# A new written-out order for an attention and gated-MLP kernel on one core, with its last half tile stored from ScalarE's queue

## The chip, the cores and the metric

The kernel runs on one core of a Trainium2 chip. The metric is the device time of one execution in microseconds, smaller is better. Before the change, three runs gave 280.32, 282.18 and 282.18, median 282.18.

## What is computed

Eight batches of twelve-head attention (448 positions, 64 per head) with RMS-normalised q and k, followed by a gated MLP over the 768 joined channels. Cut to what matters:

```python
q_n, k_n = rmsnorm(q, g_q), rmsnorm(k, g_k)
attn = softmax(q_n @ k_n.T / 8)          # per batch and head, 448 x 448
x = (attn @ v) laid out as [8, 448, 768]
h = np.maximum(x @ w_in, 0.0)            # 768 -> 1024
u, v = h[..., :512], h[..., 512:]
v_n = (v - mean(v)) / sqrt(var(v) + 1e-6)
v_s = w_spatial @ v_n + b_spatial[:, None]   # mixes the 448 positions
out = (u * v_s) @ w_out                  # 512 -> 768, float32
```

## The kernel before

A group is four heads of one batch, so there are 24 groups (0 to 23) of three per batch. A group's scores are worked out in seven units, each followed by one exponential over 128x896 numbers. Every engine does part of each group:

- SyncE's queue (SP) loads q, k and v of a group (words `l`, `L`, 224 KB or 448 KB each, into ten `raw` buffers), issues the transposing DMAs (`T`) and the stores (`t`).
- ScalarE (ACT), VectorE (DVE) and GpSimd (POOL) share squares (`q`, `Q`), normalising (`n`, `N`) and casting v (`F`); DVE sums the squares (`r`, `R`), ACT makes the reciprocal root of them with a Ln and an Exp (`i`, `j`, `I`, `J`).
- TensorE (PE) transposes the first groups (`p`, `P`), whose results an engine copies out of PSUM (`k`, `K`); later groups go through `T`, and their k through a scaling (`Z`).
- PE makes scores (`S.group.unit`, eight small matmuls that run side by side), ACT exponentiates them (`E`), and PE sums them in passes: `s` for the sums of the softmax, `a` and `b` for the two halves of attention times v. A pass serves two groups with eight small matmuls when its last number is 1, one group with four when it is 0. `D`, `d` and `X` divide.
- The MLP of a batch: `V`, `W` and `U` (times w_in), `c`, `B`, `M`, `m`, `A` (normalising), `u`, `H` and `G` (mixing and gating), `O`, `W` (times w_out), `o` (copy out of PSUM), `t` (store).
- GpSimd's queue loads the weights: `ws` the 448x448 mixing matrix, which PE transposes in four steps (`Y`), `wi` w_in in eight parts, `wo` w_out. `wb` and `wx` bring the bias. `z.n` is n matmuls without use, which only keep PE working.

No loop and no planner runs in the kernel: the string `PLAN` lists some 1640 words, and one pass over it records each word's instructions. An engine works through its own words in that order and never overtakes, and a DMA is issued when its engine's queue comes to it. A word reads `name.args/slots/engine`: `S.9.0/45` puts unit 0 of group 9 into PSUM banks 4 and 5, `E.9.0/8/a` exponentiates it on ACT into buffer 8, `Q.2.1/0/g` squares k (index 1; q is 0) of group 2 on POOL (`a` ACT, `v` DVE). Groups 0 and 1 have passes of their own, the others are summed in pairs. Three lines of the order, around groups 8 to 10:

```python
H.1.1/2 I.13//a L.15.1/1 F.8//g J.13//a E.8.4/e/a X.6.1 L.17.0/9 S.9.0/45 G.1.1 S.9.3/67 N.11.0/3/g L.10.2/2 H.1.3/3
E.9.3/2/a H.1.2/0 E.9.0/8/a G.1.3 N.13.1/0/g S.9.2/12 L.17.1/7 G.1.2 S.10.3/67 s.8.3.1/34 E.9.2/7/a T.11.0/3 s.8.0.1
R.12.1 s.8.4.1 b.8.1.1/05 s.8.1.1 E.10.3/3/a b.8.3.1 S.10.4/12 N.13.0/2/g R.14.1 b.8.5.1 s.8.5.1 E.10.4/i/a s.8.2.1
```

Of the kernel before, what the change touches and what calls it, by code (L numbers as in the profile page):

```python
# [22 lines left out]
l.0.1/0 setup l.1.1/1 l.1.0 z.32/0 gl.1//a l.0.0 gl.0//a L.1.1/2 L.1.0/3 L.3.1/4 q.0.1/0/g L.2.1/5 L.2.0/6 ws  # L23
q.1.1/1/a L.3.0/7 L.4.1/8 r.1.1 L.0.2/9 r.0.1 q.1.0//v i.1//a j.1//a n.0.1//v q.0.0//a r.1.0 p.0.1/0 gA n.1.1//v gB/1
r.0.0 p.1.1/2 gC k.0.1/0/v i.0//a z.4/3 j.0//a k.1.1/0/v n.0.0//g Q.1.0/2/a S.0.3/01 wi.1.2 L.5.0/0 p.0.0/2 Q.1.1/1/a
n.1.0//g R.1.0 z.2/3 E.0.3/0/a L.4.0/1 p.1.0/3 R.1.1 Q.3.1/0/a z.7/4 Q.2.1/2/g k.0.0//v I.1//a k.1.0//v Q.2.0/1/a
S.0.1/01 S.0.4/23 S.0.5/45 J.1//a S.0.0/67 E.0.4/1/a R.2.0 N.1.0/0/g E.0.0/2/a S.0.2/23 R.2.1 E.0.5/3/a L.6.1/3
P.1.0/6 N.1.1/1/v I.2//a E.0.2/4/a S.0.6/45 K.1.0/1/v L.1.2/2 P.1.1/7 Q.3.0/1/g E.0.6/5/a Y.3/6 K.1.1/1/v J.2//a
E.0.1/6/a R.3.1 S.1.0/23 N.2.1/2/g S.1.2/45 E.1.0/7/a Y.1/7 R.3.0 E.1.2/8/a S.1.3/01 N.2.0/3/v L.7.1/5 S.1.6/23 I.3//a
P.2.1/4 E.1.3/9/a F.0//v L.6.0/6 P.2.0/5 J.3//a Q.4.1/2/a y.1//v N.3.0/0/g K.2.1/2/v S.1.4/01 E.1.6/a/a Y.2/7 y.3//v  # L30
K.2.0/2/v E.1.4/b/a Q.4.0/0/g S.2.3/23 T.3.0/3 y.2//v b.0.3.0/4 S.1.5/56 R.4.1 E.2.3/c/a s.0.2.0/7 a.0.5.0/0 a.0.3.0
s.1.6.0/1 E.1.5/d/a s.0.1.0 L.7.0/9 S.2.1/23 Q.6.1/1/g R.4.0 s.1.2.0 s.0.0.0 L.5.1/7 E.2.1/e/a S.1.1/56 s.1.3.0
a.0.1.0 s.1.4.0 E.1.1/f/a s.1.0.0 S.2.6/23 wi.1.1 N.3.1/1/v s.0.4.0 s.0.6.0 I.4//a b.0.1.0 E.2.6/g/a S.2.4/56 a.0.4.0
s.0.3.0 F.1//v L.2.2/4 b.0.2.0 E.2.4/h/a s.1.5.0 Q.5.0/2/v s.0.5.0 L.8.0/2 a.0.0.0 b.0.4.0 S.2.0/23 J.4//a D.0/0/a
s.1.1.0 N.4.0/2/v P.3.1/5 D.1/1/a E.2.0/i/a S.2.2/67 K.3.1/3/v b.1.4.0/1 T.4.0/0 Q.6.0/0/g b.0.5.0 d.0//a b.0.6.0
R.5.0 S.3.6/23 d.1//a b.0.0.0 b.1.1.0 a.1.6.0/5 E.3.6/j/a b.1.0.0 L.3.2/1 a.1.2.0 b.1.2.0 wi.0.3 Q.7.0/2/v E.2.2/k/a
S.3.4/23 wi.0.2 a.1.5.0 a.0.2.0 X.0.1 E.3.4/l/a S.3.5/67 N.4.1/3/g a.1.1.0 R.6.1 b.1.5.0 a.1.0.0 E.3.5/4/a S.2.5/23
# [107 lines left out]
U.7.3.1 m.7//a U.7.3.0 A.7.1 A.7.0 U.7.0.0 u.7.3//a o.6.1.0//v U.7.2.2 A.7.2 O.6.2.0/3 t.6.1 A.7.3 U.7.2.0 U.7.0.2  # L145
H.7.1/0 u.7.0//a u.7.1//a H.7.3/1 o.6.2.0/0/a G.7.1 u.7.2//a H.7.0/4 G.7.3 H.7.2/0 G.7.0 O.6.2.1/1 G.7.2 o.6.2.1//a
# [595 lines left out]
```

## Time and profile before

| what | value |
|---|---|
| median of 3 runs | 282.18 us |
| profiled execution | 281.81 us; its span from the first to the last instruction 280.0 us |
| mean granted TensorE clock | 0.974 |
| PE busy | 261.3 us, 93% of the span, 4308 matmuls and as many weight loads |
| ACT busy | 219.5 us, 78% |
| DVE busy | 204.8 us, 73% |
| POOL busy | 132.0 us, 47%, none after 220 us |
| moved by DMA | 56.17 MB |

Outside the span lie 281.81 - 280.0 = 1.81 us. PE's busy share says where PE had work in its queue, not that each matmul ran at its best rate: matmuls overlap, and their ends are modelled. A line of a timeline gives the start, the length, the engine, the source line, the operation with what it writes and reads, how often, and in brackets the idle time before it with what ended it. A line of the windows gives a stretch, its length, then for PE, PEld (weight loads), DVE, ACT and POOL the busy time and in brackets the number of instructions, and at its end the granted clock of PE, the busy share of the DMA engines and GB/s.

### The profile page before, as it was taken

The numbers are of one execution on the slowest core, as the hardware profiler recorded it, in microseconds if no ns is written. First come the engines' busy times: TensorE is split into PE (matmuls) and PEld (weight loads), VectorE is DVE, ScalarE is ACT, GpSimd is POOL, SyncE is SP. The second block draws the span as 40 slices with busy tenths as digits, with TensorE's granted clock in tenths as the row PEclk, the third lists the DMA queues.
The fourth block names the chain that finished last, engine by engine and source line by source line (L and its number), as shares of the span: only waits on it lengthen the run. The fifth ranks groups of instructions, "written<-read, shape, count | busy, mean of one in ns | idle before, by whom it ended". The sixth has DMA issues, their size and how long they took to land.

```text
span 280.0 us, 10039 instructions
## 1 busy us (share of the span) xinstructions
PE 261.3 (93%) x4308; PEld 132.8 (47%) x4308; DVE 204.8 (73%) x357; ACT 219.5 (78%) x365; POOL 132.0 (47%) x99
## 2 busy tenths in 40 slices
PE   7949998699989996999999999999999999999992
PEld 3425755344434453445445545445455544555551
DVE  4659887797978887489878988897858374557640
ACT  3359999599979997599998999889789978632351
POOL 3335758469677297666795738535634000000000
PEclk9995899999999999799999999999999999999999
DMA  6995799999999999999999998899985250160346
GB/s 197 285 354 180 199 276 193 186 265 314 150 261 249 289 231 286 246 269 201 245 251 280 228 280 161 224 236 230 183 150 82 72 155 18 30 169 9 86 105 197
DMA packets 61174, 56.17 MB, mean 201 GB/s; under 512 B 37705, under 2 KB 56778, under 8 KB 61130
## 3 DMA queue, kind: packets, MB, share of 16 engines
q1 hardware_dynamic: 59618, 52.77, 79.1%
q0 software_dynamic: 1504, 2.76, 5.8%
q8 instruction: 33, 0.54, 0.8%
q14 instruction: 11, 0.09, 0.1%
q10 hardware_dynamic: 8, 0.00, 0.0%
HBM read 38.55 MB, written 11.01 MB: 177 GB/s over the span
## 4 chain that ended last, share of the span: by engine, by line
PE 82%; ACT 6%; DMA 5%; issue 3%; SPq 1%; DVE 0%; DVEq 0%; ACTq 0%
PE ps L539 16%; PE ps L506 14%; PE ps L650 14%; PE ps L584 12%; PE ps L678 12%; PE ps L664 9%; DMA raw<-in_q_dram 5%; PE ps L613 4%; ACT et L514 4%; PE ps L348 2%; PE ps L445 1%; SPq L288 1%; ACT rc L562 1%; SPq L301 1%; ACT rc L558 1%
## 5 line engine op out<-in xcount | busy, mean ns | idle before, releaser
L514 ACT ACTIVATE et<-ps 128x896 bf16<-128x896 f32 x168 | 146.7, 919 | 14.6 <-PE ps L506 13.1
L382 POOL TENSOR_TENSOR sqt<-raw 128x896 f32<-128x896 f32 (+1 forms) x33 | 54.4, 1656 | 41.0 <-DVE nrm L426 10.3
L426 POOL TENSOR_TENSOR nrm<-raw,rs 128x896 bf16<-128x896 f32 x34 | 57.0, 1688 | 31.9 <-ACT rs L411 9.2
L506 PE MATMUL ps<-qT,kT 64*32 64x448 bf16 x1344 | 57.4, 363 | 7.4 <-ACT et L514 3.5
L393 DVE TENSOR_REDUCE ss<-sqt 128x14 f32<-128x896 f32 x46 | 48.3, 1074 | 4.2 <-ACT sqt L380 4.2
L539 PE MATMUL ps<-et,vt 64*32 64x448 bf16 x1344 | 46.5, 350 | 3.5 <-issue 3.4
L650 PE MATMUL ps<-xt,w_in 128*128 128x448 bf16 x192 | 42.9, 353 | 0.0
L568 DVE TENSOR_TENSOR xt<-ps,rc 128x448 bf16<-128x448 f32 x48 | 27.9, 617 | 16.2 <-PE ps L539 8.1
L678 PE MATMUL ps<-w_out,gt 128*128 128x384 bf16 x192 | 36.9, 330 | 0.0
L584 PE MATMUL ps<-w_in,xt 128*128 128x512 bf16 x144 | 35.6, 380 | 0.0
L506 PEld LDWEIGHTS <-kT 64*32 64x32 bf16 x1344 | 19.5, 90 | 33.2 <-issue 23.0
L669 DVE TENSOR_TENSOR gt<-ps,us 128x448 bf16<-128x448 f32 x32 | 19.5, 621 | 15.0 <-PE ps L664 9.4
L539 PEld LDWEIGHTS <-vt 64*32 64x32 bf16 x1344 | 21.6, 92 | 17.4 <-issue 6.0
L664 PE MATMUL ps<-w_spT,vn 128*128 128x448 bf16 (+1 forms) x128 | 28.5, 360 | 0.0
L650 PEld LDWEIGHTS <-w_in 128*128 128x128 bf16 x192 | 17.4, 98 | 19.8 <-issue 5.7
L539 PE MATMUL ps<-et,ones 64*32 64x448 bf16 x672 | 25.0, 349 | 0.8 <-issue 0.8
L678 PEld LDWEIGHTS <-gt 128*128 128x128 bf16 x192 | 18.0, 98 | 16.2 <-issue 4.2
L361 ACT ACTIVATE os<-ps 128x384 f32<-128x384 f32 (+1 forms) x38 | 18.1, 490 | 7.8 <-PE ps L678 4.8
L625 DVE BATCH_NORM_STATS2 s<-vs 128x6 f32<-128x512 bf16 (+1 forms) x32 | 21.7, 678 | 0.5 <-ACT vs L575 0.4
L584 PEld LDWEIGHTS <-xt 128*128 128x128 bf16 x144 | 13.1, 98 | 17.7 <-issue 4.7
L577 DVE TENSOR_SCALAR vs<-ps 128x512 bf16<-128x512 f32 (+1 forms) x19 | 12.9, 686 | 9.3 <-PE ps L584 8.1
L363 DVE COPY os<-ps 128x384 f32<-128x384 f32 (+1 forms) x26 | 14.2, 552 | 7.3 <-PE ps L678 6.2
(62 smaller groups left out, 266.9 us busy)
## 6 DMA issues: line engine op xcount, KB each, us to landing
out_dram<-os SPq DMA_DIRECT2D x55, 192.0 KB, 3.0
raw<-in_k_dram SPq DMA_DIRECT2D x23, 448.0 KB, 5.4
raw<-in_q_dram SPq DMA_DIRECT2D x23, 448.0 KB, 5.5
raw<-in_v_dram SPq DMA_DIRECT2D x13, 448.0 KB, 4.9
raw<-in_v_dram SPq DMA_DIRECT2D x22, 224.0 KB, 5.1
w_in<-in_moe_w_in_dram POOLq DMA_DIRECT2D x8, 192.0 KB, 6.2
w_out<-in_moe_w_out_dram POOLq DMA_DIRECT2D x1, 768.0 KB, 10.7
raw<-in_q_dram SPq DMA_DIRECT2D x2, 224.0 KB, 3.6
```

The lines of the kernel that those rows point to most:

```text
L382: port(eng, eng.tensor_tensor(out=t, in0=x, in1=x, op=ALU.mult))
L393: dve.tensor_reduce(out=sss[G % 3][:, i].rearrange("p r c -> p (r c)"), in_=sqt[where.pop(("sq", G, i))].rearrange("p r (c d) -> p (r c) d ...
L426: port(eng, eng.tensor_tensor(out=nrm[sl[0]].rearrange("p c r d -> p r c d"), in0=raw[where["raw", G, i]].rearrange("p r (c d) -> p r c d" ...
L506: pe.matmul(out=ps[at:at + 32, sl[n], 0:S], lhsT=kT[64 * r:64 * r + 64, c, 64 * hh + 32 * x:64 * hh + 32 * x + 32], rhs=qT[64 * r:64 * r + ...
L514: act.activation(out=ets[sl[0]], in_=ps[:, a:b + 1:b - a, 0:S], func=AF.Exp, bias=0.0, scale=1.0)
L539: pe.matmul(out=ps[32 * l:32 * l + 32, where[kind, G][0], 0:S], lhsT=w, rhs=et_of(G, r, c)[at:at + 64], start=(n == 1), stop=(n == C), til ...
L568: dve.tensor_tensor(out=xts[b % 2][:, 2 * g + half, :], in0=ps[:, where.pop(("ab"[half], G))[0], 0:S], in1=rcs[where["rc", G]], op=ALU.mult)
L584: pe.matmul(out=ps[:, bank, :], lhsT=xts[b % 2][:, j, 128 * m:128 * m + 128], rhs=w_in[:, j % 2, j // 2, DH:], start=(n == 1 and j == 2 * ...
L625: dve.bn_stats(out=s6, in_=vss[b % SLOTS["vs"]][rows, m, :])
L650: pe.matmul(out=ps[:, bank, 0:S], lhsT=w_in[:, j % 2, j // 2, 128 * f:128 * f + 128], rhs=xts[b % 2][:, j, :], start=(n == 1 and j == 2 * ...
L664: pe.matmul(out=ps[:, sl[0], 0:S], lhsT=vns[b % SLOTS["vn"]][rows, m, 128 * f:128 * f + 128], rhs=w_spT[rows, m, :], start=(m == 0), stop= ...
L678: pe.matmul(out=ps[:, sl[0], 0:384], lhsT=gts[b % 2][:, f, 128 * m:128 * m + 128], rhs=w_out[:, f, 384 * h:384 * h + 384], start=(f == 0), ...
```

## The change

The whole of `PLAN` is another one: the same scores, exponentials, passes and MLP steps, in another order on every engine, with other PSUM banks and buffers, and with some steps on other engines. Counted over the two orders:

| step | before | after |
|---|---|---|
| idle-filling matmuls `z` | 45 (32 + 4 + 2 + 7) | 41 (26 + 4 + 4 + 2 + 3 + 2) |
| whole tiles that PE transposes (`P`), by DMA (`T`) | 8, 38 | 9, 37 |
| `u` (relu of u) on ACT, on DVE | 17, 15 | 11, 21 |
| squares `Q` on ACT, DVE, POOL | 9, 5, 32 | 11, 6, 29 |
| normalising `N` on DVE, POOL | 12, 34 | 14, 32 |
| casts of v `F` on ACT, DVE, POOL | 1, 10, 13 | 1, 6, 17 |

The first lines of the order, before and after, and the lines around the passes of groups 8 and 9 after:

```diff
-l.0.1/0 setup l.1.1/1 l.1.0 z.32/0 gl.1//a l.0.0 gl.0//a L.1.1/2 L.1.0/3 L.3.1/4 q.0.1/0/g L.2.1/5 L.2.0/6 ws
-q.1.1/1/a L.3.0/7 L.4.1/8 r.1.1 L.0.2/9 r.0.1 q.1.0//v i.1//a j.1//a n.0.1//v q.0.0//a r.1.0 p.0.1/0 gA n.1.1//v gB/1
+l.0.1/0 setup l.1.0/1 l.1.1 z.26/0 gl.0//a l.0.0 gl.1//a L.1.1/2 L.1.0/3 q.0.1/0/a L.2.1/4 L.2.0/5 r.0.1 L.0.2/6
+q.1.0/1/g L.4.0/7 wb/0 q.1.1//a L.3.0/8 r.1.1 L.3.1/9 r.1.0 i.1//a j.1//a gA q.0.0//a n.0.1//v r.0.0 p.0.1/0 n.1.1//v
...
+o.1.0.1/4/v s.8.5.1/12 N.12.1/3/g s.8.6.1 E.9.0/1/a s.8.2.1 X.6.0 S.10.0/34 s.8.3.1 s.8.4.1 E.10.0/d/a s.8.1.1
+a.8.4.1/05 s.8.0.1 b.8.6.1/67 Q.14.0/2/v T.12.1/1 b.8.5.1 D.9/0/a S.10.5/34 a.8.5.1 D.8/1/a a.8.1.1 b.8.1.1 Z.11/3/v
+d.9//a b.8.3.1 b.8.2.1 L.14.1/8 a.8.6.1 E.10.5/h/a N.13.0/2/g b.8.4.1 b.8.0.1 T.12.0/0 a.8.3.1 a.8.2.1 X.9.1 d.8//a
...
-W.8/02 t.6.2 O.7.0.0/1 o.7.3.1/4/a o.7.3.0//a O.7.0.1/3 o.7.0.0/3/v t.7.3 O.7.2.0/0 o.7.0.1//a O.7.2.1/1 o.7.2.0/1/a
-t.7.0 O.7.1.0/2 o.7.2.1//a O.7.1.1/0 o.7.1.0/2/a t.7.2 o.7.1.1//v t.7.1
+o.7.3.1//a O.7.1.0/2 t.7.3//a O.7.2.0/0 o.7.1.0//a o.7.2.1/4/a t.7.1 o.7.2.0//v t.7.2
```

In the code, a load in two halves and a store in two halves can name two queues, and the last tile's second half goes to the queue that the word names (ACT for `t.7.3//a`); an operation `op_h` is added that no word of the order uses.

```diff
-            engines[e or "s"].dma_start(out=raw[sl[0]][64 * half:64 * half + 64], in_=src)
+            engines[(e or "ss")[half]].dma_start(out=raw[sl[0]][64 * half:64 * half + 64], in_=src)
...
-            for at in sorted({tail_at(b, 0), tail_at(b, 1)}):
+            for n, at in enumerate(sorted({tail_at(b, 0), tail_at(b, 1)})):
...
-                sync.dma_start(out=out_c[b][6][:, cols], in_=t[at:at + 64, cols])
+                engines[(e or 's') if n else 's'].dma_start(out=out_c[b][6][:, cols], in_=t[at:at + 64, cols])
```

At the start, SP's queue before and after (`raw` is the buffer, then what is loaded; line 301 and 306 are half loads `l`, the others whole ones `L`). Before:

```order
L301 DMA raw_64<-in_q_dram 128x448
L301 DMA raw_65<-in_k_dram 128x448 x2
L288 DMA raw_66<-in_k_dram 128x2x448
L288 DMA raw_67<-in_q_dram 128x2x448
L288 DMA raw_68<-in_k_dram 128x2x448
L288 DMA raw_69<-in_k_dram 128x2x448
L288 DMA raw_70<-in_q_dram 128x2x448
L288 DMA raw_71<-in_q_dram 128x2x448
```

After:

```order
L306 DMA raw_64<-in_q_dram 128x448
L306 DMA raw_65<-in_k_dram 128x448 x2
L293 DMA raw_66<-in_k_dram 128x2x448
L293 DMA raw_67<-in_q_dram 128x2x448
L293 DMA raw_68<-in_k_dram 128x2x448
L293 DMA raw_69<-in_q_dram 128x2x448
L293 DMA raw_70<-in_v_dram 128x2x448
L293 DMA raw_71<-in_q_dram 128x2x448
```

The two loads of group 2 (k into raw_69 and q into raw_70 before; raw_68 and raw_69 after) move up by one place, past k of group 3. The halves of group 0's k change places. On POOL, `ws` moves from behind the first square to behind the square of group 2's k, and the first `wi` behind the normalising of group 1's q.

ACT's queue from the squares of group 1 on (line 380 and 385 squares, 514 and 519 exponentials, 406 and 411 or 411 and 416 the Ln and Exp, 467 a copy of a transposed tile). Before:

```order
L380 ACTIVATE sqt_76<-raw_67 128x896
L380 ACTIVATE sqt_75<-raw_66 128x896
L514 ACTIVATE et_91<-ps 128x896
L380 ACTIVATE sqt_74<-raw_68 128x896
L406 ACTIVATE ls_119<-ss_116,eps 128x28
L380 ACTIVATE sqt_75<-raw_70 128x896
L411 ACTIVATE rs_122<-ls_119 128x28
L514 ACTIVATE et_92<-ps 128x896
L514 ACTIVATE et_93<-ps 128x896
L514 ACTIVATE et_94<-ps 128x896
```

After:

```order
L385 ACTIVATE sqt_76<-raw_66 128x896
L385 ACTIVATE sqt_75<-raw_67 128x896
L519 ACTIVATE et_91<-ps 128x896
L411 ACTIVATE ls_119<-ss_116,eps 128x28
L519 ACTIVATE et_92<-ps 128x896
L416 ACTIVATE rs_122<-ls_119 128x28
L385 ACTIVATE sqt_76<-raw_69 128x896
L519 ACTIVATE et_93<-ps 128x896
L519 ACTIVATE et_94<-ps 128x896
L519 ACTIVATE et_95<-ps 128x896
L411 ACTIVATE ls_120<-ss_117,eps 128x28
L467 ACTIVATE kT_88<-ps,g_col 128x896
```

The square of group 3's k (raw_68 before) is no longer ahead of the second exponential, and one copy out of PSUM comes to ACT.

SP's queue around the passes of groups 8 and 9 (line 288 and 293 loads, 481 and 486 transposing DMAs, 702 and 707 stores of a tile, 704 of a half tile). Before:

```order
L481 DMA_TRANSPOSE kr_85<-nrm_78 128x7x128
L288 DMA raw_65<-in_k_dram 128x2x448
L288 DMA raw_73<-in_q_dram 128x2x448
L288 DMA raw_66<-in_v_dram 128x2x448
L288 DMA raw_71<-in_k_dram 128x2x448
L481 DMA_TRANSPOSE qT_84<-nrm_80 128x7x128
L481 DMA_TRANSPOSE qT_81<-nrm_79 128x7x128
```

After:

```order
L486 DMA_TRANSPOSE kr_85<-nrm_79 128x7x128
L704 DMA out_dram<-os_143 64x768
L486 DMA_TRANSPOSE qT_84<-nrm_78 128x7x128
L707 DMA out_dram<-os_140 64x768 x2
L486 DMA_TRANSPOSE kr_86<-nrm_80 128x7x128
L293 DMA raw_72<-in_k_dram 128x2x448
L486 DMA_TRANSPOSE qT_81<-nrm_77 128x7x128
```

Four loads stood ahead of the transposes there; now two stores of finished tiles do, one load stands among the transposes and the next loads behind them.

More of the change, by code (lines that the diff above doesn't have):

```diff
@@ L28 @@
[L28 to L37, printed above, removed]
@@ L254, in op_z, with op_h @@
                       rhs=ident[:, None, 0:T].to_broadcast([128, C, T]), start=True, stop=True)
+    def op_h(sl, e, n):
+        for _ in range(n):
+            pe.matmul(out=ps[:, 7, S:512], lhsT=ident, rhs=ident[:, 0:T], start=True, stop=True)
     where = {}
```

232 lines of the change are left out of this document (120 added, 112 removed).

## The prediction

> **What bounds the kernel now.** I read the page first (PE 93% busy), then a table of ten-microsecond stretches, then the chain of waits, and last the timeline of the two ends.
>
> ```profile
> 120.00:130.00 10.00, 10.00 (x108) 4.51 (x106) 8.56 (x15) 9.85 (x18) 6.94 (x5) 1.00 0.97 231
> 250.00:260.00 10.00, 10.00 (x59) 5.17 (x58) 5.59 (x10) 2.06 (x4) 0.00 (x0) 1.00 0.25 66
> ```
>
> From 120 us on PE is busy 10.00 of 10 at the full clock, almost to the end: whatever the order, that work takes what it takes, and ACT (9.85 of 10 beside it) leaves little room either. An order can win at four places: the first 25 us, single waits of PE up to 116 us, a clock that falls to half, and the last 10 us. The single waits are these, in the chain:
>
> ```profile
> 47.64 0.84 issue
> 52.09 2.31 issue
> 76.78 1.11 issue
> 110.11 2.12 issue
> ```
>
> "Issue" means that no semaphore explains them. Stretches cut at them, and the page's row for fetched instructions, do:
>
> ```profile
> q8 instruction: 33, 0.54, 0.8%
> 0.00:42.04 42.04, 35.86 (x477) 19.95 (x478) 29.49 (x48) 29.23 (x47) 20.52 (x23) 0.88 0.87 248
> 42.04:48.47 6.43, 5.60 (x134) 3.55 (x129) 4.80 (x8) 6.32 (x11) 5.64 (x7) 1.00 1.10 199
> 48.47:54.39 5.92, 3.58 (x128) 1.84 (x128) 4.84 (x6) 3.17 (x5) 1.93 (x2) 1.00 1.03 131
> 54.39:71.07 16.68, 16.52 (x247) 7.58 (x254) 14.54 (x27) 15.09 (x26) 12.73 (x9) 1.00 1.12 282
> 71.07:77.89 6.82, 5.71 (x145) 2.78 (x130) 6.03 (x9) 6.82 (x13) 5.39 (x4) 1.00 1.26 146
> 77.89:106.05 28.16, 28.15 (x506) 13.52 (x513) 24.34 (x42) 25.84 (x43) 18.82 (x14) 1.00 1.13 268
> 106.05:112.22 6.17, 3.39 (x144) 1.96 (x130) 4.30 (x7) 4.05 (x7) 4.12 (x4) 0.98 1.20 278
> 155.80:159.97 4.17, 4.17 (x122) 2.40 (x127) 4.11 (x8) 4.17 (x12) 2.66 (x2) 1.00 1.17 188
> 211.25:214.77 3.52, 3.52 (x124) 1.96 (x130) 2.45 (x6) 3.52 (x6) 1.77 (x2) 1.00 0.43 66
> 112.03:115.44 3.41, 3.21 (x16) 1.31 (x16) 0.00 (x0) 1.73 (x4) 3.25 (x3) 0.50 0.98 271
> ```
>
> Between one such wait and the next lie 128, 384 (254 + 130) and 643 weight loads, multiples of 128 but for 3. The page has 33 packets of instructions; 4308 pairs of load and matmul over 33 is 131. So PE's program comes in pieces of 128 pairs, and PE stops at an edge when the next piece isn't there. The four pieces that ended in a stop took 6.43, 5.92, 6.82 and 6.17 us, on average 6.34: so long did a fetch take there. Others took 4.17 with busy DMA engines (share 1.17) and 3.52 with quiet ones (0.43) without a stop. A stop therefore needs two things: a piece with little PE time in it, and a slow fetch. The four stops sum to 0.84 + 2.31 + 1.11 + 2.79 = 7.05 us (the last is 112.23 less the end of the last pass, 107.93 + 1.51, below), and right at the last the clock stood at half for 3.41 us.
>
> [...]
>
> **The start.** In the first 25 us ACT waits for loads, and everything behind it on its queue with it:
>
> ```profile
> 6.28 0.62 DVE L382 TENSOR_TENSOR sqt<-raw 128x448 f32<-128x448 f32 x1 [0.58 <-DMA raw<-in_k_dram]
> 9.60 0.21 ACT L419 ACTIVATE rs<-ls 128x14 f32<-128x14 f32 x1
> 12.46 1.79 ACT L380 ACTIVATE sqt<-raw 128x896 f32<-128x896 f32 x2 [2.65 <-DMA raw<-in_q_dram]
> 12.57 0.56 PE L506 MATMUL ps<-qT,kT 64*32 64x448 bf16 x8 [0.26 <-DVE kT L464]
> 13.45 2.08 DVE L393 TENSOR_REDUCE ss<-sqt 128x14 f32<-128x896 f32 x2 [0.93 <-ACT sqt L380]
> 16.01 0.95 ACT L380 ACTIVATE sqt<-raw 128x896 f32<-128x896 f32 x1 [0.95 <-DMA raw<-in_k_dram]
> 17.86 1.68 POOL L382 TENSOR_TENSOR sqt<-raw 128x896 f32<-128x896 f32 x1 [5.50 <-DMA raw<-in_k_dram]
> 19.02 0.95 ACT L380 ACTIVATE sqt<-raw 128x896 f32<-128x896 f32 x1 [1.85 <-DMA raw<-in_q_dram]
> 19.99 2.51 ACT L514 ACTIVATE et<-ps 128x896 bf16<-128x896 f32 x3
> 20.94 0.94 PE L506 MATMUL ps<-qT,kT 64*32 64x448 bf16 x8 [3.15 <-ACT et L514]
> 22.59 1.74 ACT L514 ACTIVATE et<-ps 128x896 bf16<-128x896 f32 x2
> 8.00:11.50 3.50, 3.50 (x29) 2.12 (x27) 1.72 (x5) 0.52 (x2) 1.58 (x3) 1.00 1.00 235
> 16.50:20.00 3.50, 0.97 (x32) 0.53 (x33) 0.26 (x1) 1.65 (x5) 1.68 (x1) 0.98 1.07 377
> gt<-in_moe_w_spatial_dram POOLq DMA_DIRECT2D x1, 392.0 KB, 10.9
> ```
>
> The second exponential waits at 19.99 behind two squares whose loads (the seventh and the ninth of SP) landed at 16.0 and 19.0, and PE waits 3.15 us for its bank. By then the sixth exponential ends at 24.33 (22.59 + 1.74). Two causes are in the rows: 392 KB of `ws` share the engines for 10.9 us (235 GB/s at 8 to 11.5 us, against 377 without it), and k of group 3 stands ahead of group 2.
>
> After, neither does. The queue's steps with these durations: the third half load is now k's second half, 6.3; square on ACT 0.58, reduce 0.6, Ln and Exp 0.5: 8.1. Normalise q, reduce and normalise k on DVE: 10.1; transpose, copies: first scores at 12.1, near the 12.57 of before. DVE then does two reduces (2.08), two copies (1.2): second scores at 15.3 (16.82 before). The load of group 2's q: 448 KB at 377 GB/s take 1.2 us, so from a fourth half load at 6.9 the fourth whole one lands at about 12. Its square ends on ACT at 16.1, then three exponentials (2.51), a Ln (0.3), the added copy out of PSUM (0.95), an Exp, the sixth exponential: 20.7 us, 3.6 ahead. That is the upper bound. If the load lands as the eighth one did before, 17.86, the square starts 2.6 us later and 1.0 is left. Scores that come late at half clock can cost about 0.8 of either, so the lower bound is 0.2. From there on ACT has the same squares to do as before up to the pairs (five either way), so the lead is kept while ACT sets the pace. I take **-2.8**, near the upper end, since `ws` is what the rows blame.
>
> On that half clock: the stretch 19.87 to 30.11 has PE busy and the clock at half all the same.
>
> ```profile
> 19.87:30.11 10.24, 9.15 (x106) 5.41 (x105) 9.25 (x13) 9.71 (x17) 6.26 (x4) 0.50 0.69 216
> ```
>
> [...]
>
> **The fetches.** Counted along the new order in the same pieces, at full clock, with prices from these rows:
>
> ```profile
> 105.66 0.37 PE L539 MATMUL ps<-et,ones 64*32 64x448 bf16 x8
> 107.93 1.51 PE L539 MATMUL ps<-et,vt 64*32 64x448 bf16 x56
> ```
>
> One paired pass of eight small matmuls takes 0.37 us and seven take 1.51, so each further one adds 0.19; scores, as many matmuls again, count the same or a little more (0.23), the other steps by their own rows. Before, three pieces are thin (12 to 14 passes and 2 to 4 scores, 3.1 us each), from weight loads 609, 1633 and 3425 of the program on; two of them ended in the stops of 2.31 and 2.79. After, the same three are as thin (3.12, 3.09, 3.16), and two more come: from load 2657 (15 passes, one score: 3.08; 4.4 before) and 3681 (3.33). The piece from 993 falls from 5.2 to 4.5, from 481 from 4.9 to 4.6, from 1377 from 4.2 to 3.8. So by the count alone the new order is worse. What speaks for it are the transfers: ahead of the piece from 1633 stood four loads of 448 KB, now two stores; the last two `wi` stand half a piece earlier against the one from 609. But transposing DMAs stand at both.
>
> Bounds: with quiet engines (3.52) the five thin pieces cost 0.40 + 0.43 + 0.44 + 0.36 + 0.19 = 1.8 us, 5.2 less than 7.05. With fetches of 6.34 at the six pieces up to load 2784 they cost 3.2 + 3.25 + 3.25 + 1.9 + 1.7 + 2.5 = 15.9, and the two late ones 0.55: 9.4 more. I take 5.5, 1.4 at each of the three thin early pieces and 1.3 for the rest: **-1.5**.
>
> **The end, and small things.**
>
> ```profile
> 269.28 0.62 DVE L669 TENSOR_TENSOR gt<-ps,us 128x448 bf16<-128x448 f32 x1 [0.21 <-PE ps L664]
> 269.96 0.84 PE L613 MATMUL ps<-w_out,gt 128*64 128x384 bf16 x8
> 271.86 1.10 SPq L699 DMA_DIRECT2D out_dram<-os  x2
> 273.07 3.74 SPq L702 DMA_DIRECT2D out_dram<-os  x6
> 274.90 0.56 DVE L363 COPY os<-ps 128x384 f32<-128x384 f32 x1 [2.75 <-PE ps L678]
> ```
>
> PE waits 0.68 us (269.28 to 269.96) for the last gating; after, two output steps of batch 6 (0.65 each) stand there and hide it: -0.7. The half store on ACT's queue spares SP one issue, 0.55 us (1.10 for two), but SP's last stores start behind the last copies anyway (274.90 + 0.56), and the issue now stands on ACT ahead of the last two copies there, which the last two stores wait for: +0.4 (0 to 0.9). Together **-0.3**. One more tile that PE transposes is seven matmuls, 0.84 us by the row below if nothing hides them: **+0.5**, between 0 and 0.84; six fewer relu on ACT and six more on DVE lie under PE's work, since both are below 9.9 of 10 where they stand; uncovered they would cost about the 0.56 of a copy of that size each.
>
> ```profile
> 27.94 1.68 PE L445 MATMUL ps<-ident,nrm 128*128 128x128 bf16 x14
> ```
>
> **Sum**, against the profiled execution: 281.81 - 2.8 - 1.5 - 0.3 + 0.5 = **277.7 us**. The median of the runs, 282.18, is 0.4 above it; I leave the sum as it is.
>
> **The rivals.** (a) Fetches as before: the fewer loads help no more than the thinner pieces hurt, 7.05 stays, and the sum is 279.2. For it speaks the slow fetch of 42.04 to 48.47, beside one transpose and the weights. (b) Slower: fetches set the time. The transposes at the thin pieces keep them at 6.34, all six early pieces stop PE, +9.4 instead of -1.5, 281.81 + 9.4 - 2.8 - 0.3 + 0.5 = 288.6; with the shortest of the four slow fetches, 5.92, the same pieces give 13.9, +6.8 and 286.0. I put it at 286.5. It decides once the stops sum to more than 12.5 us (7.05 + 2.6 + 2.8). Against it: the piece of 4.17 at share 1.17. (c) The start doesn't do what its order says: the loads of group 2 land as late as before, 0.2 is left of 2.8, and the sum is 280.3.
>
> **How the numbers follow.** A measurement of this kernel tells about 1% from no change, so faster means under 279.4 and slower over 285.0. My forecast has 0.45, of which 0.38 lies under 279.4; (a) 0.20, half and half; (b) 0.22, all slower but 0.01; (c) 0.13, of which 0.04 is faster. That makes 0.52 faster, 0.26 same, 0.22 slower. The forecast's own range is 272.5 to 281 (fetches at best -5.2 and start at best -3.6 give 273; fetches at 7.05 and start at 1.0, 281). The range has to hold (a), (c) and most of (b): 271 to 286.5.
>
> **What would show it.** Right: the sixth exponential ends near 20.7; no DMA wait of ACT over 1 us after 13 us; stops of "issue" on PE at the same loads with a sum near 5.5; no gap of PE ahead of the last output steps. Wrong: squares of group 2 at 18 us or later; a stop over 2 us at load 1633 or 2657; a stretch at half clock after 40 us; PE waiting for a transposed k or q, for which I have no term.

## The result, and the profile after

The changed kernel takes 279.77 us (median of 16 runs, 277.23 to 283.26), the kernel before beside it 286.91 us (16 runs, 280.32 to 294.16). Some executions of the kernel before are several per cent longer than its others (a wait that such executions have is shown below); the ratio leaves those out, the medians don't. The ratio is 0.9886, 95% interval 0.9847 to 0.9926: 1.1% faster, where the prediction had 277.7 against 282.18, 1.6%. Profile against profile it is 278.61 us for 281.81, span 276.8 for 280.0.

The page after, in the rows that answer to those of before: the engines, the clock, and the packets of instructions.

```profile
PE 260.8 (94%) x4311; PEld 131.6 (48%) x4311; DVE 210.7 (76%) x364; ACT 220.0 (79%) x361; POOL 126.6 (46%) x97
PEclk9999799999999999999999999999999999999999
q8 instruction: 33, 0.54, 0.9%
```

PE does the same work (260.8 us busy, 261.3 before) in a span 3.2 us shorter. The stretches (busy time of PE, PEld, DVE, ACT and POOL, granted clock, DMA share, GB/s) show where the half clock stands now, and two stretches that are full in both kernels:

```profile
19.87:30.11 10.24, 9.24 (x178) 6.30 (x177) 9.34 (x13) 9.82 (x16) 5.48 (x4) 1.00 0.71 198
30.17:33.58 3.41, 3.32 (x42) 1.67 (x36) 2.54 (x4) 3.41 (x6) 3.39 (x4) 0.50 0.93 205
120.00:130.00 10.00, 10.00 (x150) 4.47 (x148) 9.84 (x19) 9.10 (x18) 5.34 (x4) 1.00 0.84 229
250.00:260.00 10.00, 10.00 (x60) 5.28 (x59) 7.44 (x16) 3.78 (x9) 0.00 (x0) 1.00 0.09 20
```

The waits of PE between 16 and 260 us, in two tables: total, number of waits, longest. First of the kernel before, then of the changed one.

```profile
PE ps L539 <- issue: 4.3, 3, 2.3
PE ps L506 <- ACT et L514: 3.5, 3, 3.1
PE ps L506 <- issue: 2.8, 1, 2.8
```

```profile
PE ps L544 <- issue: 3.6, 4, 1.5
PE ps L511 <- ACT et L519: 0.8, 3, 0.3
PE ps L669 <- issue: 0.7, 1, 0.7
```

The wait of 3.1 us for the second exponential is gone, and the waits that no semaphore explains fell from 7.1 us to 4.3. The chain of waits places four of the five that are left:

```profile
49.22 1.54 issue
74.15 0.77 issue
97.80 0.70 issue
108.23 0.93 issue
```

They end at the weight loads 736, 1120, 1504 and 1760 of the program, the fifth (0.37) at 2784: each 32 short of a multiple of 128, at multiples of 128 from one another.

To see where the lead comes from and goes, I summed PE's steps in each kernel's own order at their prices at full clock (0.19 us for eight small matmuls, and so on, fillers left out), and read from both traces when so much work was done. The leads are estimates: with 0.19 or 0.23 us for a score step they move by up to half a microsecond.

| work done (us at full clock) | before | after | lead |
|---|---|---|---|
| 10 | 32.5 | 27.9 | 4.6 |
| 14 | 36.5 | 34.0 | 2.5 |
| 35 | 64.3 | 60.8 | 3.6 |
| 70 | 103.5 | 100.4 | 3.1 |
| 80 | 118.3 | 112.3 | 6.0 |
| 215 | 260.6 | 256.5 | 4.0 |
| PE's end | 274.8 | 271.1 | 3.8 |
| end of the span | 280.0 | 276.8 | 3.2 |

Four readings follow. The start brings PE 4.6 us, and 2 of them are gone by 14 us of work, where the half clock at 30.17 stands. The half clock is at most a part of that: ACT is busy for 3.41 of 3.41 us there, and ACT's own lead, counted in exponentials done, goes from 3.4 us at the ninth to 2.2 at the seventeenth; its first wait for PE after 22 us, 0.72 us, ends only at 34.68. Up to 35 us of work 1.6 us of the lead come from the stops (3.15 before, 1.55 after), so the start has kept 2.0. Between 70 and 80 the lead grows by 2.9: the kernel before has its stop of 2.79 us there, the changed one 0.93, and about 1.0 is left for the 3.41 us of half clock behind the longer stop. Then 2 us are given back on the way to 215, where I had no term; 0.37 of them is the fifth stop.

The end, on the timeline of the changed kernel:

```profile
264.81 3.41 PE L683 MATMUL ps<-w_out,gt 128*128 128x384 bf16 x20
268.16 0.84 PE L618 MATMUL ps<-w_out,gt 128*64 128x384 bf16 x8
269.92 0.56 ACTq L704 DMA_DIRECT2D out_dram<-os  x1
270.58 0.87 ACT L366 ACTIVATE os<-ps 128x384 f32<-128x384 f32 x2 [0.69 <-PE ps L683]
271.09 2.39 SPq L707 DMA_DIRECT2D out_dram<-os  x4
```

PE goes from step to step without the gap of 0.68 us ahead of the last gating; the copies on ACT come after ACT's own issue, but their wait of 0.69 us is put down to PE, and four stores start as the copies run. From PE's end to the end of the span it is 5.8 us, 5.2 before.

### The profile page after: what moved, and what is told of

It reads as the page before. It is cut to its first block, busy times and chain, and to the rows that moved or that the text cites. A ratio compares the mean times of both kernels' runs of the same rounds, so it can differ in the third digit from the quotient of the medians.

```text
span 276.8 us, 10039 instructions
## 1 busy us (share of the span) xinstructions
PE 260.8 (94%) x4311; PEld 131.6 (48%) x4311; DVE 210.7 (76%) x364; ACT 220.0 (79%) x361; POOL 126.6 (46%) x97
## 3 DMA queue, kind: packets, MB, share of 16 engines
q0 software_dynamic: 1504, 2.76, 5.8%
## 4 chain that ended last, share of the span: by engine, by line
PE 77%; DMA 9%; DVE 4%; issue 3%; ACT 2%; SPq 1%; POOL 1%; DVEq 0%
PE ps L544 16%; PE ps L511 12%; PE ps L655 12%; PE ps L683 11%; PE ps L589 10%; PE ps L669 9%; DMA raw<-in_k_dram 5%; PE ps L618 4%; DMA raw<-in_v_dram 2%; DMA kr<-nrm 2%; ACT et L519 2%; DVE ss L398 1%; DVE nrm L431 1%; PE ps L353 1%; PE ps L450 1%
## 5 line engine op out<-in xcount | busy, mean ns | idle before, releaser
L431 POOL TENSOR_TENSOR nrm<-raw,rs 128x896 bf16<-128x896 f32 x32 | 53.6, 1687 | 35.7 <-ACT rs L416 10.7
L387 POOL TENSOR_TENSOR sqt<-raw 128x896 f32<-128x896 f32 (+1 forms) x30 | 49.4, 1653 | 23.5 <-DVE kT L469 5.1
L544 PE MATMUL ps<-et,vt 64*32 64x448 bf16 x1344 | 47.9, 351 | 3.6 <-issue 3.6
L655 PE MATMUL ps<-xt,w_in 128*128 128x448 bf16 x192 | 42.0, 353 | 0.0
L573 DVE TENSOR_TENSOR xt<-ps,rc 128x448 bf16<-128x448 f32 x48 | 27.9, 617 | 18.5 <-ACT rc L567 9.2
L589 PE MATMUL ps<-w_in,xt 128*128 128x512 bf16 x144 | 37.1, 380 | 0.0
L511 PEld LDWEIGHTS <-kT 64*32 64x32 bf16 x1344 | 20.2, 90 | 31.3 <-issue 21.3
L321 POOL CAST vt<-raw 128x896 bf16<-128x896 f32 x17 | 15.7, 931 | 37.0 <-PE ps L669 21.7
L669 PE MATMUL ps<-w_spT,vn 128*128 128x448 bf16 (+1 forms) x128 | 27.8, 353 | 0.7 <-issue 0.7
L544 PE MATMUL ps<-et,ones 64*32 64x448 bf16 x672 | 26.0, 349 | 0.0
L368 DVE COPY os<-ps 128x384 f32<-128x384 f32 (+1 forms) x27 | 15.0, 555 | 11.5 <-PE ps L683 9.2
```

Source lines behind the costliest of these rows:

```text
L387: port(eng, eng.tensor_tensor(out=t, in0=x, in1=x, op=ALU.mult))
L431: port(eng, eng.tensor_tensor(out=nrm[sl[0]].rearrange("p c r d -> p r c d"), in0=raw[where["raw", G, i]].rearrange("p r (c d) -> p r c d" ...
L511: pe.matmul(out=ps[at:at + 32, sl[n], 0:S], lhsT=kT[64 * r:64 * r + 64, c, 64 * hh + 32 * x:64 * hh + 32 * x + 32], rhs=qT[64 * r:64 * r + ...
L544: pe.matmul(out=ps[32 * l:32 * l + 32, where[kind, G][0], 0:S], lhsT=w, rhs=et_of(G, r, c)[at:at + 64], start=(n == 1), stop=(n == C), til ...
L573: dve.tensor_tensor(out=xts[b % 2][:, 2 * g + half, :], in0=ps[:, where.pop(("ab"[half], G))[0], 0:S], in1=rcs[where["rc", G]], op=ALU.mult)
L589: pe.matmul(out=ps[:, bank, :], lhsT=xts[b % 2][:, j, 128 * m:128 * m + 128], rhs=w_in[:, j % 2, j // 2, DH:], start=(n == 1 and j == 2 * ...
```

## The experiments

Medians are of the kernel's own runs; "stops" are PE's waits at an edge of a 128-pair piece in the profiled execution, "half clock" the time at 0.50 before 260 us there. The ratio is to the kernel before on the same chip, with its interval, where one could be formed. Four chips were used, and the kernel before itself differs between them, so rows of different chips compare by their ratios.

| kernel | chip | median us (n) | ratio | stops us | half clock us |
|---|---|---|---|---|---|
| before, again | 1 | 285.02 (4) | 1.011 (1.002-1.021) | 6.5 | 13.7 |
| before, new loads | 1 | 284.63 (4) | none | 6.0 | 13.7 |
| before, transpose first | 2 | 282.89 (12) | 0.995 (0.990-1.000) | 5.6 | 10.2 |
| before, shift 60 | 13 | 280.00 (12) | 0.989 (0.979-0.998) | 0.8 | 17.1 |
| before, fillers inside | 13 | 282.17 (12) | 0.998 (0.990-1.006) | 2.0 | 6.8 |
| before, three edits | 6 | 277.20 (12) | 0.988 (0.983-0.993) | 2.1 | 10.2 |
| after, again | 2 | 279.44 (6) | 0.989 (0.983-0.996) | 2.7 | 10.2 |
| after, `ws` early | 1 | 279.19 (4) | 0.990 (0.981-0.999) | 4.0 | 10.2 |
| after, store on SP | 1 | 280.04 (10) | 0.990 (0.983-0.996) | 4.9 | 6.8 |
| after, fillers inside | 13 | 276.80 (12) | 0.996 (0.991-1.001) | 1.5 | 3.4 |
| after, shift 0 | 2 | 280.57 (6) | none | 3.8 | 3.4 |
| after, shift 92 | 13 | 273.32 (6) | 0.979 (0.971-0.987) | 0.9 | 6.8 |
| after, shift 92, again | 2 | 274.79 (6) | 0.973 (0.967-0.979) | 0.4 | 3.4 |
| after, shift 116 | 6 | 280.51 (6) | none | 3.1 | 3.4 |
| after, shift 92, Y.0 later | 6 | 276.62 (6) | 0.987 (0.978-0.996) | 1.4 | 6.8 |

### The kernel before, unchanged

> The kernel before, unchanged, profiled once more. If its waits at the edges of the instruction pieces are a fixed property of the order, PE stops again at weight loads 609, 737, 1121 and 1761, with a sum near 7.05 us and a span near 280. If they depend on how long each fetch happens to queue behind data, the same thin pieces stop for other lengths, the sum moves by 2 us or more, and the span moves with it. Ratio 1.00 either way.

It stopped 1.65 us at load 736, 1.04 at 1120, 2.79 at 1760 and, new, 1.01 near 3168; the one at 609 did not come. The last is a lesson in reading:

```profile
198.02 0.11 PEld L506 LDWEIGHTS <-kT 64*32 64x32 bf16 x8 [1.45 <-issue]
198.02 0.38 PE L506 MATMUL ps<-qT,kT 64*32 64x448 bf16 x8 [1.01 <-ACT et L514]
```

The matmul's wait is put down to an exponential, but its weight load waited longer for nothing that the profile shows, and a packet of instructions ended 1.4 us ahead. The sum is 6.5 us at partly other edges, the span 283.4, with 13.65 us of half clock in one piece (21.33 to 34.98). So the order sets where PE can stop, the fetch of the moment whether and how long. The kernel measured against itself gave 1.011: a per cent in such a ratio is no evidence by itself, and agreement between kernels has to carry it.

### The loads of the start: alone in the old order, and half undone in the new

```diff
 kernel before: l.0.1/0 ... L.1.1/2 L.1.0/3
-L.3.1/4 q.0.1/0/g L.2.1/5 L.2.0/6 ws
+q.0.1/0/g L.2.1/5 L.2.0/6 L.3.1/4
-n.1.0//g R.1.0
+n.1.0//g ws R.1.0
```

> The kernel before, with two words moved: `ws` behind the normalisation n.1.0 on POOL's queue (issued near 12.4 us, not 4.4), and the load L.3.1 behind both loads of group 2. Nothing else. Theory (the loads of the first 12 us set the start, as the term of 2.8 us says): the squares of group 2 start by 16 us, PE's wait of 3.1 us for the second exponential shrinks below 1, the sixth exponential ends near 21.5, and the time falls by 2 to 3 us, ratio 0.990 to 0.993. Rival (the lead is lost behind the half clock and ACT's full queue): the sixth exponential is early, but the time falls by less than 1 us, ratio over 0.997.

```diff
 changed kernel
-q.1.0/1/g L.4.0/7
+q.1.0/1/g ws L.4.0/7
-k.1.0//v ws J.1//a
+k.1.0//v J.1//a
```

> The changed kernel, with `ws` put back to the place it had before: POOL's first load, behind the square q.1.0. Theory (`ws` takes the DMA engines from the loads of groups 1 and 2): those loads land 2 us or more later, the sixth exponential ends at 23 us or later instead of 21.2, and the time grows by 1.5 to 3 us over the changed kernel. Rival (the order of SP's own loads is what counts): the sixth exponential moves by less than 0.7 us and the time by less than 0.7.

The exponentials on ACT's timeline: the third to sixth of the old order with the new loads.

```profile
17.86 1.71 ACT L514 ACTIVATE et<-ps 128x896 bf16<-128x896 f32 x2
19.67 1.73 ACT L514 ACTIVATE et<-ps 128x896 bf16<-128x896 f32 x2
```

The two move the sixth exponential from 24.33 to 21.4 us, 2.9 earlier, and at 40 us of work the kernel is 4.5 us ahead of the first profile of before (65.3 against 69.85). That the start gains what the prediction said is confirmed, in a kernel that has only the start. It did not become a gain in time: this execution then waited 8.4 us for a transposing DMA (next part). The four runs are 275.95, 282.85, 286.42 and 286.88; the shortest is below all fourteen of the kernel before on that chip (278.75 and more), but it is one run.

The sixth exponential of the changed kernel, and that of the one with `ws` early again:

```profile
20.34 0.90 ACT L519 ACTIVATE et<-ps 128x896 bf16<-128x896 f32 x1
```

```profile
21.11 0.91 ACT L519 ACTIVATE et<-ps 128x896 bf16<-128x896 f32 x1
```

They end at 21.24 and 22.01. That is 0.8 us, nearer to the rival, and the time did not move (0.990 and 0.989). So of the 3 us at the sixth exponential `ws` makes about 0.8 in the new order. If the two add up, the order of SP's own loads makes the rest; that order alone was not tried.

### Who waits at 70 us: the transposing DMA

```diff
 kernel before
-L.10.0/6 V.0.1.2 ... c.0.2//v L.10.1/5 I.8//a ... L.11.1/9 U.0.2.2/4 ... T.7.0/3
+V.0.1.2 ... c.0.2//v I.8//a ... U.0.2.2/4 ... T.7.0/3 L.10.0/6 L.10.1/5 L.11.1/9
```

> The kernel before with the three loads L.10.0, L.10.1 and L.11.1 (448 KB each) moved behind the transposing DMA T.7.0 on SP's queue. In some executions of the kernel before that transpose lands 14 to 17 us after its issue and PE waits 5.7 to 8.4 us for it near 70 us; in the one first profiled PE did not wait. Theory (it queues behind the 1.3 MB issued just ahead of it): it lands within 8 us, PE never waits over 1 us between 68 and 80, and the times over 285 us are gone: median 4 us or more under that of the kernel before, fast executions within 1%. Rival (the transpose is slow by itself, or behind the others that are under way): the spread stays, 276 to 290.

What it is about, in the chain of waits and then the waits of PE of the kernel before with its edges shifted by 60 pairs:

```profile
62.94 13.95 DMA qT<-nrm
```

```profile
PE ps L511 <- DMA qT<-nrm: 5.8, 1, 5.8
```

T.7.0, issued at 62.94, reaches PE at 76.9. With the new loads it took 17.1 us and PE waited 8.4, with fillers inside 5.7; 6.83 us of half clock begin in each of these waits. In the two profiles of the kernel before unchanged PE used it 9.4 and 10.4 us after its issue, and waited 0 and 1.0 us. With the three loads behind it, PE's longest wait for such a DMA is 0.3 us:

```profile
PE ps L506 <- issue: 3.6, 1, 3.6
PE ps L539 <- issue: 1.3, 1, 1.3
PE ps L506 <- DMA qT<-nrm: 0.3, 1, 0.3
```

The median is 282.89 against 287.46 for the kernel before on the same chip, and the slowest run 286.06 against 293.19. The theory holds but for its last number: three of twelve runs are still over 285 (285.30, 285.98 and 286.06). The ratio is 0.995 (0.990 to 1.000): the edit does next to nothing for the executions without that wait. In the changed kernel T.7.0 goes out at 66.6, when the load ahead of it has landed (63.0) and the next three stand behind it, lands 3.5 us later, at 70.1, and is used at 74.9; no profile of it or of its variants shows this wait. For the medians (286.91 to 279.77) this is the largest single thing that the change did, if the 4.6 us here are its measure, and neither the prediction nor the first profile contained it, because that execution had escaped it. For the ratio of 0.9886 it is not.

### The edges: shifts by 0, 60, 92 and 116 pairs

```diff
 changed kernel, shift 92 (shift 0: h.16; shift 116: h.132)
-z.26/0
+z.10/0 h.108
 kernel before, shift 60, with op_h taken over
-z.32/0
+z.14/0 h.78
```

The fillers h are matmuls of 64 columns in PE's wait for the first load. They don't touch the order; they move PE's program against the pieces.

> The changed kernel with 92 pairs of load and matmul more ahead of PE's first real work (16 of the 26 fillers z at the start become 108 fillers of 64 columns, in the wait for the first load), so that every edge of a 128-pair piece falls 92 pairs earlier in the work. Nothing else moves. Theory (a stop is a thin piece that meets a slow fetch): counted with the prices of the passes, the thin pieces of 3.1 us at loads 736, 1504 and 1760 become pieces of 3.7 us or more, and the sum of the stops falls from 4.3 us to 2 to 3; those that stay are at other places of the work. Time 1 to 2 us under the changed kernel. Rival (stops come from the transfers at their time, not from the edges): the stops stay where they are in the work, within 0.5 us of the same sum.

> The changed kernel, unchanged, as the base for its neighbours on the same chip. If stops depend on how each fetch happens to queue, its profile shows again four to six stops at the edges from loads 736, 1120, 1504, 1760 and 2784, with a sum between 3 and 6 us (4.3 in the first profile). Ratio to the kernel before 0.985 to 0.992, as measured.

> Control: the changed kernel with the start's 26 fillers z replaced by 10 z and 16 fillers of 64 columns, so the edges stay where they were, but the first 8 us of PE look like those of the kernel shifted by 92. Theory (the edges are what shifted): same as the changed kernel within 0.7 us, same places of the stops. Rival (the shorter filler, and the clock it leaves, is what helped the shifted kernel): 2 us or more under the changed kernel.

> The shifted kernel once more, now beside the changed kernel on one chip. Its profile had stops of 0.94 us in all, the changed kernel 4.32. Theory: 2.5 to 3.5 us under the changed kernel, stops under 2 us in this profile too. Rival (a chip that happened to be quick): less than 1 us under it.

> The changed kernel with 116 pairs more ahead of PE's first real work (10 z and 132 fillers of 64 columns), 24 more than in the kernel shifted by 92. Theory (it is where the edges fall, not the filler, nor a later or earlier start): by the count of the pieces the thin ones of 3.0 to 3.1 us are back, at three early and two late places, so the stops sum to 2.5 us or more again and the time is within 1.5 us of the changed kernel's 279.4, 4 above the shift by 92. Rival (more fillers at the start help by themselves): 276 or less, stops under 1.5.

The waits of PE at edges: the changed kernel again, then shift 92 on the same chip, then shift 116 in its chain.

```profile
PE ps L544 <- issue: 1.4, 3, 0.5
PE ps L669 <- issue: 1.4, 1, 1.4
```

```profile
PE ps L511 <- issue: 0.4, 1, 0.4
```

```profile
49.12 1.16 issue
97.80 0.76 issue
164.39 0.80 issue
```

On one chip the changed kernel takes 279.44 (six runs, 278.11 to 285.50), its control with shift 0 takes 280.57 (275.66 to 283.83), and shift 92 takes 274.79 (273.10 to 276.24): 4.7 us less for moving nothing but the edges. It was expected to bring 2.5 to 3.5. The changed kernel stopped 2.7 us this time, a little under the 3 to 6 expected. The control was to lie within 0.7 of the changed kernel and lies 1.1 above it, on the side that speaks against the filler. The first shift 92, on another chip, was to keep 2 to 3 us of stops and kept 0.9.

At 24 pairs more, on a third chip, the stops are back at other places (3.1 us), which speaks against the filler and the wait it stands in. The time, 280.51, says less: two of the six runs are short (275.61 and the profiled one, 277.21), the other four are 279.80 to 283.51. The profiled spans of the changed kernel and its control (276.3 and 277.5) and of shift 92 (273.0 and 271.3) agree with the medians. Of the 4.8 us between their averages 2.6 are the stops themselves (3.3 and 0.7; the 0.9 of the first shift 92 is put down to DVE by its waits, but stands at an edge). The start differs by up to 1.6 us between these executions, with no edge to blame, and the rest is spread, so 2.6 of the 4.7 us are shown to be stops and the others are not placed. Shift 92 beats both kernels: ratio 0.979 and 0.973.

The count of the pieces was less good than its idea. With a fetch of 5.4 us up to 95 us of work and 4.4 after (the author's estimates; the five pieces that ended in a stop in the first profile of the changed kernel took 3.8 to 5.7 us), it gives 10.5 us of stops to the changed kernel (measured 2.7 to 4.3), 6.6 to shift 92 (0.4 to 0.9) and 11.9 to shift 116 (3.1). It tells shift 92 from the other two, at three times the size or more, and it fails for the 32 pairs of the fillers below (10.2 against 1.5). In the old order it failed too: shifted by 60, the stops at 736 and 1120 were to stay within 0.7 of 2.3 and 1.1 and did not come at all, and the one at 1760 was to shrink below 0.5 and took 0.82. The fetch of the moment is not in a count.

### The half clock

```diff
 changed kernel, fillers inside
+h.8 behind each of P.2.1/7, Y.1/6, Y.3/7, Y.0/2
 kernel before, fillers inside
+h.36 behind S.0.0/67; h.8 behind each of P.1.1/7, Y.3/6, Y.1/7
 changed kernel, shift 92, Y.0 later
-Y.0/2 y.3//v ... y.0//v ... z.2/4
+y.3//v ... Y.0/4 y.0//v
```

> The changed kernel with four times eight fillers of 64 columns behind P.2.1, Y.1, Y.3 and Y.0, the transposes that PE makes between 24.9 and 29.4 us. [...] Rival (ACT sets the pace there): the half clock goes, the time falls by less than 0.5. A second rival (PE's time of 32 fillers, about 1.3 us, costs more than it saves): slower by 0.5 to 1.

> The kernel before with 60 pairs more ahead of PE's first real work (18 of 32 fillers z become 78 of 64 columns). Control for the next one: its edges fall at the same places of the work. By the count of the pieces the stop behind the last load of k (2.79 us at load 1760) shrinks below 0.5 and the ones at loads 736 and 1120 stay within 0.7 of 2.3 and 1.1; the time falls by 1 to 2 us. The half clock from 20 to 30 us or longer stays.

> The kernel before with 60 fillers of 64 columns inside the start instead: 36 in PE's wait ahead of S.0.2 (17.8 to 20.9 us), eight each behind P.1.1, Y.3 and Y.1. Edges behind 28 us as in the control. Theory (much of the gain of the changed kernel is the clock: 13.7 us at half before, 3.4 after): the half clock of 20 to 30 us shrinks to one window of 3.41 us or none, the work done by 35 us comes 1.5 to 2.5 us earlier than in the control, and the time is 1.5 to 2.5 us under it. Rival (the loads and ACT set the pace until 30 us, as the prediction had it): the half clock goes and the time stays within 0.8 of the control.

> The kernel shifted by 92, with one of the four transposed pieces of w_spatial, Y.0, moved from 28 us to 48 us (in place of the filler z.2), where no transpose of PE stands. In all executions of the changed kernel one to three windows of half clock follow 27.5 us. Theory (the transposes of 24.9 to 29.4 bring it, and it costs what the first profile showed, about 2 us of the lead): the half clock after 27 us is gone or one window shorter, and the time is 1 to 2 us under the 273 to 275 of the shifted kernel. Rival (ACT sets the pace there and the loss is made up later): within 0.7 of it.

In the old order the test is clean: the control has half clock where the one with fillers has none.

```profile
19.64:29.88 10.24, 9.83 (x116) 6.08 (x116) 9.07 (x13) 9.71 (x16) 6.54 (x5) 0.50 0.81 275
```

```profile
19.64:29.88 10.24, 8.58 (x159) 6.36 (x155) 8.71 (x14) 9.05 (x15) 5.89 (x5) 1.00 0.75 262
```

By 14 us of work the kernel at full clock is 0.7 us ahead (34.9 against 35.6), by 27 it is 0.3 ahead (51.7, 52.0), and its median is 2 us higher, not lower (282.17 and 280.00). ACT is over 9 of 10.24 us busy in both rows: there PE's clock costs next to nothing, as the prediction had assumed. Whether the 2 us are a difference at all isn't settled: the intervals of the two ratios overlap, and the profiled executions are 0.4 us apart (283.95 and 283.57).

In the new order the half clock from 30.17 was to go and did not. With 32 fillers the window from 25.85 was full of PE work (3.41 of 3.42 us), and the next ran at half all the same:

```profile
25.85:29.27 3.42, 3.41 (x61) 2.86 (x60) 1.09 (x1) 2.93 (x5) 1.76 (x2) 1.00 0.17 47
29.27:32.68 3.41, 3.14 (x50) 1.32 (x49) 3.15 (x6) 2.58 (x4) 1.81 (x3) 0.50 0.95 220
```

Its 276.80 are no evidence on the clock, since 32 pairs more also moved the edges (stops 1.5 us), and the kernel before is quick on that chip too (ratio 0.996). With Y.0 moved away the half clock is 6.83 us (30.37 to 37.20), where the two profiles of the shifted kernel have 6.83 and 3.41, and the time is 276.62, above the two medians of the shifted kernel, but on another chip. So what exactly brings the half clock behind 27 us stays open. What it costs shows in two profiles of the changed kernel: after 10.24 us of it (the second) the work of 24 us is done 1.8 us later than after 3.41 (48.3 and 46.5), the work of 65 us 0.5 later (94.7 and 94.2), most of it made up by the stop that follows, 0.41 instead of 1.55 us.

### The half store

```diff
 changed kernel
-t.7.3//a O.7.2.0/0 o.7.1.0//a o.7.2.1/4/a t.7.1
+O.7.2.0/0 o.7.1.0//a o.7.2.1/4/a t.7.3 t.7.1
```

> The changed kernel, with the half tile t.7.3 stored by SP alone, in front of t.7.1. My term says ScalarE's issue costs 0.4 us, because the last copies wait behind it: without it the copy o.7.1.0 starts 0.5 us earlier and the distance from PE's end to the end of the span falls from 5.75 to about 5.3. Rival: SP's one issue more (0.55 us) delays the last stores by as much, and the distance stays within 0.2 of 5.75.

```profile
271.33 1.12 SPq L704 DMA_DIRECT2D out_dram<-os  x2
272.11 0.87 ACT L366 ACTIVATE os<-ps 128x384 f32<-128x384 f32 x2 [0.56 <-PE ps L683]
272.62 2.40 SPq L707 DMA_DIRECT2D out_dram<-os  x4
```

SP is busy with the two halves until 272.45 and issues the last four stores from 272.62 on, as the last copies start (272.11, 272.76), just as before. From PE's end to the end of the span: 5.7 us, 5.8 with the half on ACT. The rival holds; which engine stores that half is worth 0.1.

### Three edits in the old order

```diff
 kernel before
-z.32/0
+z.14/0 h.78
-L.3.1/4 q.0.1/0/g L.2.1/5 L.2.0/6 ws
+q.0.1/0/g L.2.1/5 L.2.0/6 L.3.1/4
-n.1.0//g R.1.0
+n.1.0//g ws R.1.0
-L.10.0/6 V.0.1.2 ... L.10.1/5 I.8//a ... L.11.1/9 U.0.2.2/4 ... T.7.0/3
+V.0.1.2 ... I.8//a ... U.0.2.2/4 ... T.7.0/3 L.10.0/6 L.10.1/5 L.11.1/9
```

> The kernel before with three single edits together: the loads of the start (as tried alone), the three loads behind the transposing DMA T.7.0 (as tried alone), and 60 pairs more ahead of the first real work (as tried alone). If the early loads, the late transpose and the edges are what sets the two kernels apart, this gives the changed kernel's time with the old order of everything else: sixth exponential near 21.5, no wait over 1 us at 70 to 80 us, stops under 3 us, median 277 to 280. Rival (the new order of scores and passes itself is worth something): 281.5 or more.

Median 277.20 us, ratio 0.988 (0.983 to 0.993); the changed kernel has 0.989. The sixth exponential ends at 21.33, no wait of PE at 70 to 80 us is over 0.6, and what PE waits for now is this:

```profile
PE ps L544 <- DVE vt L321: 2.0, 1, 2.0
PE ps L511 <- issue: 1.6, 2, 1.1
PE ps L544 <- issue: 0.5, 1, 0.5
```

Three edits of a handful of words give the old order the ratio that the new one has, and a like fall of the median beside the kernel before: 8.0 us here (285.16 to 277.20), 8.0 for the changed kernel on another chip (287.46 to 279.44). How the 1.1% divide among the three is not shown: the shift by 60 alone had 0.989, with a wide interval. One wait is left that no profile of the new order has, 2.0 us for a cast of v (the first line).

That is not to say that the rest of the new order is worth nothing. Its edges were not moved here, the old order's were; with its own edges moved by 92 the new order has 0.979 and 0.973, and the old order was tried at one shift only.

## Why the prediction was right or wrong

**What bounds the kernel.** Right, and stronger than written: PE stops at edges of 128 pairs, where a thin piece (3.1 to 5.2 us by the count at the four stops of the first profile of before) meets a slow fetch (which started there 3.6 to 4.6 us after the edge ahead). The shifts show the edges by moving them alone; that it takes a thin piece is shown less well, since the count of thin pieces failed for two of the shifts. PE stands 4.3 us at edges in the changed kernel, and a shift by 92 pairs takes 2.6 us of stops away.

**The start, -2.8.** The queue's steps came out: sixth exponential at 21.24 for 20.7, 3.1 us ahead of before. Two reasons were off. `ws` is 0.8 of it and not the main thing, and the lead was not kept "while ACT sets the pace": it rose to 4.6 us and was 2.5 behind a half clock at 30.17, with ACT full; net of the stops 2.0 arrive. For the half clock the sum had no term. The one at 20 to 30 us is gone (1.00 in that stretch, 0.50 before), and a new one stands at 30.17, behind Y.1, Y.3, Y.0 and P.2.1, which the new order puts together at 24.9 to 29.4 us. That these transposes bring it is not shown: neither fillers among them nor one of them fewer took it away.

**The fetches, -1.5.** The mechanism was right, the size a little small: 4.32 us in the profile for the predicted 5.5, 2.73 less than before, and 2.7 us in another execution. The stops named for the thin pieces from 609, 1633 and 2657 came (1.55, 0.93, 0.37), the ones from 3425 and 3681 passed without one, as rows with quiet queues had promised (2.85 and 3.3 us long; the next pieces had landed 0.2 and 1.5 us after the crossing). By the count alone the new order is worse, and that the transfers decide was the right choice. Rival (b), 12.5 us of stops, was far off: fetches of 6.34 us at every early piece did not come.

**The end, -0.3.** The gap ahead of the last gating is gone (-0.7) and PE's end to the span's end grew by 0.6: together -0.1. But the half store on ACT is hardly why it grew; on SP it is 5.7, against 5.8. After the change four stores are issued from the last copies on (2.39 us of SP), where before SP issued its last six without a break from 273.07 on (3.74 us), ahead of the last copy at 274.90.

**One P more, +0.5, and relu.** No wait stands there in the profile that could be put down to them; I can't say more.

**What failed.** The step that failed is the sentence "From 120 us on PE is busy 10.00 of 10 at the full clock, almost to the end: whatever the order, that work takes what it takes". Its price was zero; the profiles lose 2 us there, and the sum had 4.1 us off the profiled execution (281.81 to 277.7) where 3.2 came (278.61). From 80 to 215 us of work the first profile of before took 142.2 us and the changed kernel 144.2, and the fifteen others of both orders 143.1 to 147.1. So the base of my sum was the shortest execution of all in that stretch, by luck: it has no stop after 115 us, where three other profiles of the old order stop 0.7 to 1.4 us near load 3168. What else the others lose there stays open. The other mis-sized term is the start, 2.0 for 2.8. The terms give, as measured: start -2.0, stops -2.7, half clock at 112 to 115 us about -1.0 (no term), the late stretch beside its stop of 0.37 +1.6 (no term), PE's end to the end of the span +0.6, small remainders +0.3: -3.2, as in the spans. That the sum came near is partly luck, since the stops fell by 1.2 us more than forecast and the half clock had no term.

The chances were added up a little off: by the parts named, "same" has 0.27 and "slower" 0.21.

**What was never in it.** The wait for T.7.0. I had listed "PE waiting for a transposed k or q, for which I have no term" as something that would make the prediction wrong. The wait was in executions of the kernel before, in no profile of the new one.

## What to carry to other kernels

Where a long straight program keeps PE busy, count its matmuls modulo the piece of instructions (128 pairs of load and matmul here): fillers in an idle stretch, which cost nothing that these runs show, may be worth as much as a search over orders (a shift by 92 pairs brought 4.7 us here), and any edit ahead shifts all edges behind it, so compare orders at several shifts before believing one. Take a second and a third profile of the base before summing against it, and look at the range of its times: a spread of 5% in one kernel (280.32 to 294.16) and 2% in the other (277.23 to 283.26) went here with a wait that only some executions of the first have. A transposing DMA that PE needs soon should not stand behind loads such as the three of 448 KB here: with them ahead of T.7.0 PE waited 5.7 to 8.4 us for it in three executions, with them behind it no more than 0.3.

## What the runs showed of the hardware

- A fetch of a 16 KB piece is one packet of 0.9 to 1.2 us mostly (up to 2.6), but in the first two profiles it starts between 3.0 us before and 4.6 us after PE's first weight load behind the edge ahead of it. After 200 us, where the queues go quiet (DMA share 0.22 at 210 to 220 us of the changed kernel), it starts at most 1.5 us after; in the long delays (3.2 to 4.6 us) 0.5 to 1.6 MB of other packets moved. At a stop PE goes on 1.2 to 1.6 us after the packet's end.
- Up to 260 us the half clock came in multiples of 3.41 us, and in the same kernel one to three of them (3.41 and 10.24 us in two profiles of the changed one). In the first profile after, a window with scores and passes in 0.96 of its 3.41 us (from 23.34) was followed by full clock, the next one, with 1.31 of 3.42 us, by half; with the fillers inside, a window in which PE was busy 3.41 of 3.42 us (from 25.85) was followed by half too. In these profiles the share of such work in the window just before doesn't tell it.
- The transposing DMA T.7.0 took 3.5 us from issue to landing with no load ahead of it under way, and 5.4 and 4.9 us in the two profiles with the three loads of 448 KB moved behind it. Behind them, PE used it 9.4, 10.4, 13.3, 14.0 and 17.1 us after its issue in five profiles.
